# First batch of a Fourier-mixing kernel: six row chunks of 126 instead of eight of 95

## Chip, cores and metric

The kernel runs on one core of a Trainium2 chip. The metric is the device time of one execution in microseconds (us); the median of five runs is compared. The engines are called as the profile calls them: PE (TensorE matmul), PEld (its weight loads), DVE (VectorE), ACT (ScalarE), POOL (GpSimd), SP (SyncE, which here only issues transfers).

## What is computed

The real part of a two-dimensional Fourier transform of each of eight batches, and then a two-layer network with a leaky ReLU on every token. All is float32; the two weight matrices arrive as float64 and are converted on the chip.

```python
B, S, D, F = 8, 3008, 256, 2048
X = np.fft.fft(x, axis=1)             # x: (8, 3008, 256)
X = np.fft.fft(X, axis=2).real        # -> (24064, 256) tokens
h = X.reshape(B * S, D) @ w_in        # (256, 2048)
g = np.maximum(0.01 * h, h)
out = g @ w_out                       # (2048, 256)
```

## The kernel before

**Units and steps.** Output positions k along the sequence are split by parity; a unit is (batch, parity c), odd positions (c = 1) before even ones (c = 0): (0, 1), (0, 0), (1, 1) and so on. Each unit has three column blocks of about 251, and each block is raised to the hidden width and brought down again in eight steps. A step is `up` (`raised`: four matmuls of 251 columns, L738; `activate`: DVE L747, L751 and L752, ACT's leaky ReLU L753, and from the third block on four POOL operations, L760 to L763) and, three steps later, `down` (seven matmuls, L811; for the first two blocks eight plain ones, L791). The feature transform is folded into w_in (`fold_w_in`, L516).

**The sequence transform.** The rows of x are folded by symmetry on DVE (`add_mirrors` L287, `fold_columns` L294 and L296, `fold_halves` L303). Then each unit has a cosine and a sine part. In each, the even rows and the odd rows are multiplied with tables of cosines or sines, and a butterfly of sums and differences on DVE makes the tile `mix` that L738 reads. With 95 rows to a chunk x stands in eight chunks, four for the even and four for the odd rows. A third, small transform of eight columns does the Nyquist feature of all batches; its row is stored to DRAM (`store_nyquist`) and loaded back spread over all partitions (`nb`). It is transformed once for each parity.

**Two kinds of transform.** All units but the first run `fold_rows` (24 operations on DVE and four on ACT for both parts together) and then `dft`: `even_rows` and `odd_rows`, eight matmuls of about 95 columns (L572). The first unit, (0, 1), leaves out those folds: the class `Direct` multiplies the chunks with larger tables of their own (`even_rows` L390: 94, 94, 188 and 188 columns; `odd_rows` L399: four matmuls of 376 columns, for the two parts cut at column 251 into 251 and 125). Unit (0, 0) takes the first way; its two transforms stand in steps 18 and 21 (`step`, `f in (2, 5)`).

**Order at the start.** PE, DVE and SP run in an order written out by hand until step 15; after that a scheduler places the instructions. `keep_warm(n)` issues n matmuls of 256 columns on a blank tile. PE's order at the start: 16 keep_warm, `fold_w_in` (four matmuls, L516), even Nyquist rows, 3 keep_warm, even cosine rows, odd Nyquist rows, 3 keep_warm, even sine rows, odd rows of both parts (251 columns), `spread_first` (L706), two `raised`, odd rows (125 columns), and the first `down`. On DVE `o.begin()` (L463 and L464), the first operations on a freshly loaded piece of w_out, stands ahead of the butterflies of the odd rows; `o.end()` (L482) makes that piece ready for the first `down`.

**Transfers.** SP issues, in order: w_in, the Nyquist rows, x (even rows, two halves, with the feature table between), tables, x (odd rows, two halves, with tables between), tables, pieces of w_out and w_in, and the eight ordinary tables. After each `fold_w_in` piece one row of the result is spread into `wn` by four small transfers; those of the first piece go through ACT's queue, and L747 reads them. SP's and ACT's transfers take eight completion counters in turn, so the issue of one waits until the one that had its counter before has landed.

**Buffers.** The banks of tag "up" (four of 512 columns) hold the transforms' products and those of `raised`; x has one buffer, so batch 1 is loaded when unit (0, 0)'s products have read batch 0. The tags "s" (four buffers) and "g" (five) hold the direct tables at the start and the activations later.

Of the kernel before, what the change touches and what calls it, by code (L numbers as in the profile page):

```python
# [55 lines left out]
F32 = mybir.dt.float32  # L58
I32 = mybir.dt.int32
U32 = mybir.dt.uint32  # L60
ALU = mybir.AluOpType
# [3 lines left out]
P = 128  # L65
# [3 lines left out]
NT = 8  # L69
# [10 lines left out]

DW = [6 * KB[1], 8 * KB[1], 8 * KB[1]]

# [17 lines left out]


def k_order(c):


    if c == 1:
        below = 4 * np.arange(1, KB[1] + 1) - 1
        k = np.concatenate([below, S // 8 - below])
        return np.concatenate([k, Q - k])
    first = np.concatenate([8 * np.arange(KB[0]) + 2, [188], 8 * np.arange(23) + 4, 8 * np.arange(24)[::-1]])
    k = np.concatenate([first, S // 8 - first[first != 188]])  # L110
    return np.concatenate([k, Q - k[:-1]])


def laid_out(x):

    rows = row_order()
    none = rows < 0
    d = np.concatenate([np.arange(P + 1), np.arange(D - 1, P, -1)])  # L120
    x = np.concatenate([x, np.zeros((B, 1, D), x.dtype)], axis=1)

    def taken(rows, d):
        return x[:, np.where(none, S, rows % S)][..., d]

    mirrored = (D - d) % D
    x = np.stack([
        np.stack([taken(rows, d), taken(S - rows, mirrored)], axis=2),
        np.stack([taken(H - rows, d), taken(H + rows, mirrored)], axis=2),
    ], axis=2)  # L130
    nyquist = x[..., P].transpose(1, 2, 3, 4, 0).copy()
    x[..., P] = 0.0
    x = x.reshape(*x.shape[:4], 2, NT // 2, D).transpose(0, 2, 4, 1, 3, 5, 6)
    return x, nyquist


def seq_tables():


    out = np.zeros((4, 2, LOADED, TW[0][1]), np.float32)  # L140
    direct_out = np.zeros((2, LOADED, sum(DW)), np.float32)
    rows = row_order()

    def values(chunk, k):

# [16 lines left out]
    for part in range(2):  # L162
# [19 lines left out]
        out[2 * part + 1, 0, :, : TW[0][1]] = np.concatenate([values(4, fours)[part], values(4, eights)[part], p, q], axis=1)  # L182
        k = k_order(1)
        direct_out[part] = np.concatenate(
            [values(i, k[: KB[1] * (1 + i // 2)])[part] for i in range(4)] + [values(i, k)[part] for i in range(4, NT)], axis=1)
    return out, direct_out
# [52 lines left out]
def tile_fnet_leaky_relu(  # L239
    ctx: ExitStack,  # L240
    tc: tile.TileContext,
    x: bass.AP,
    x_nyq: bass.AP,
    w_in: bass.AP,
    w_out: bass.AP,
    seq_tab: bass.AP,
    direct_tab: bass.AP,
    angle_tab: bass.AP,
# [14 lines left out]
    def dft_ps():  # L263
        return up_ps("dft_ps")
# [14 lines left out]
    def load_rows(t, b, h, odd):  # L279
        nc.sync.dma_start(t[:, h, :, odd * NI[0] : NI[0] + odd * NI[1]], x[b, h, odd])  # L280

    zs = {}
# [51 lines left out]
    class Rows:  # L334
# [3 lines left out]
        def __init__(self, src, scratch, part, c):  # L338
            self.src, self.scratch, self.part, self.c = src[0:ROWS], scratch, part, c
# [40 lines left out]
    class Direct:  # L380


        def __init__(self, src, part, tab):
            self.src, self.part, self.tab, self.c = src[0:ROWS], part, tab, 1

        def even_rows(self, m):

            pe, n, at = dft_ps(), KB[1], 0
            for i, (lo, hi) in enumerate(((0, n), (n, 2 * n), (2 * n, 4 * n), (2 * n, 4 * n))):
                nc.tensor.matmul(pe[0:m, lo:hi], lhsT=self.src[:, i], rhs=self.tab[0][0:ROWS, at : at + hi - lo],  # L390
                                 start=(i == 0), stop=(i == 3), skip_group_check=True)
                at += hi - lo
            return pe

        def odd_rows(self, m, lo=0, hi=KW[1]):

            po, n = dft_ps() if m == P else sum_ps(), KW[1]
            for i in range(4):
                nc.tensor.matmul(po[0:m, 0 : hi - lo], lhsT=self.src[:, 4 + i],  # L399
                                 rhs=self.tab[1 + i // 2][0:ROWS, i % 2 * n + lo : i % 2 * n + hi], start=(i == 0), stop=(i == 3))  # L400
            return po
# [15 lines left out]
    nyx = const.tile([LOADED, 2, 2, NT, B], F32, name="nyx")  # L417
    nyz = const.tile([LOADED, 16, B], F32, name="nyz")
    angle = const.tile([LOADED, 6], F32, name="angle")
    inf = const.tile([P, 2], F32, name="inf")  # L420
# [155 lines left out]
    def butterfly(to, m, part, c, v=nc.vector, direct=False):  # L576
# [34 lines left out]
        def even(pe):  # L611
            if direct:
                e0, pe = copied(pe, 0, n)
                v.tensor_tensor(ab[0:m, 0:n], e0[0:m, 0:n], pe[0:m, n : 2 * n], op=ALU.add)
                either(ab[0:m, n : 2 * n], e0[0:m, 0:n], pe[0:m, n : 2 * n])
                v.tensor_tensor(ev[0:m, 0 : 2 * n], ab[0:m, 0 : 2 * n], pe[0:m, 2 * n : 4 * n], op=ALU.add)
                either(ev[0:m, 2 * n : 4 * n], ab[0:m, 0 : 2 * n], pe[0:m, 2 * n : 4 * n])
                return
# [15 lines left out]

        def added(po, lo=0, hi=kw):
            nc.vector.tensor_tensor(to[0:m, lo:hi], ev[0:m, lo:hi], po[0:m, 0 : hi - lo], op=ALU.add)

        def subtracted(po, lo=0, hi=kw):
            nc.vector.tensor_tensor(to[0:m, kw + lo : kw + hi], ev[0:m, lo:hi], po[0:m, 0 : hi - lo], op=ALU.subtract)

# [39 lines left out]

    def fold_nyquist():
        nc.gpsimd.tensor_tensor(nyb, nya, nyb, op=ALU.add)
        nc.gpsimd.tensor_tensor(nya[:, 1], nyb[:, 0], nyb[:, 1], op=ALU.subtract)
        nc.gpsimd.tensor_tensor(nya[:, 0], nyb[:, 0], nyb[:, 1], op=ALU.add)

# [156 lines left out]
    def step(at):  # L842
        if at < len(steps):
# [3 lines left out]
            b, c = units[n]  # L847
            if n == 0 and f in (2, 5):
                dft(units[1], f // 5)
            if 0 < n < len(units) - 1:  # L850
# [23 lines left out]
    with tc.manual_schedule(engines={mybir.EngineType.DVE, mybir.EngineType.PE, mybir.EngineType.SP}):  # L874
        with tc.manual_schedule(engines={mybir.EngineType.Pool, mybir.EngineType.Activation}):
# [6 lines left out]
            t = x_tile()  # L882
            evens, odds = slice(0, NI[0]), slice(NI[0], NT)


            touched = const.tile([P, 1], F32, name="touched")
            nc.scalar.dma_start(touched, x[0, 0, 0, :, 0, 0, 0:1])

            nc.scalar.activation(lrelu, inf[:, 0:1], ACT.Lrelu)
            w = load_w_in(0, WN)  # L890
            nc.sync.dma_start(nyx, x_nyq)
            load_rows(t, 0, 0, 0)
            nc.sync.dma_start(feat_sb, feat_tab.rearrange("(a p) n -> p a n", p=P))
            load_rows(t, 0, 1, 0)
            tables = [[work.tile([P, 2 * WN], F32, tag=tag, bufs=bufs, name="direct") for tag, bufs in (("s", 4), ("g", 5), ("g", 5))]
                      for _ in range(2)]

            def load_direct(part, pieces):
                for i in pieces:
                    at = sum(DW[:i])  # L900
                    nc.sync.dma_start(tables[part][i][0:LOADED, 0 : DW[i]], direct_tab[part, :, at : at + DW[i]])

            load_direct(0, (0,))
            load_rows(t, 0, 0, 1)
            load_direct(0, (1, 2))
            load_rows(t, 0, 1, 1)
            load_direct(1, range(3))
# [7 lines left out]
            convert(w)  # L915
            fold_nyquist()
            differences = work.tile([P, 2 * WN], F32, tag="s", bufs=4, name="differences")[0:LOADED].rearrange("p (c d) -> p c d", d=P)
            cosine, sine = (Direct(src, part, tables[part]) for part, src in enumerate((differences, t[:, 0, 0, :, P:D])))
            nyq = Direct(nya[:, 1], 0, tables[0])
            for h in range(2):  # L920
# [24 lines left out]
            made_nyq[0](even_nyq)  # L945
            keep_warm(3)
            made = [mix(u, part, direct=True) for part in range(2)]
# [3 lines left out]
            made_nyq[1](odd_nyq)  # L951
            keep_warm(3)
            made[1][0](sine.even_rows(P))
# [18 lines left out]
        with tc.manual_schedule(engines={mybir.EngineType.Activation}):  # L972
# [16 lines left out]
            convert_on(o2, o3)  # L989
            w2 += load_w_in(2 * WN, WN, (1,))  # L990
            o4, o5 = load_w_out(4), load_w_out(5)
            up(*steps[4])
# [10 lines left out]
            fold_w_in(2 * WN, WN, w2)  # L1003
            o6, o7 = load_w_out(6), load_w_out(7)
            for at, old, new in ((8, o4, o5), (9, o5, w3[0]), (10, w3[0], w3[1]), (11, w3[1], o6), (12, o6, o7), (13, o7, None), (14, None, None), (15, None, None)):
                if old is not None:
# [8 lines left out]
                else:  # L1015
                    down(*steps[at - 2])
                if at == 14:
                    nyq = Rows(nya[:, 0], [nyz], 0, 0)
                    nyq.fold_even(nc.gpsimd)
                    nyq.fold_odd(nc.gpsimd)  # L1020
                    for part in range(2):
                        fold_halves(t, part, 0, slice(0, NT))
        done = 14
        for part in range(2):
            fold_rows(units[1], part)
    nyq_t = nyquist_tile()
    for made, bank in zip(butterfly(nyq_t, B, 0, 0), (even_rows(nyq, B), odd_rows(nyq, B))):
        made(bank)
    store_nyquist(0, nyq_t)
    spread(units[1])  # L1030
    for f in range(0, NH, WB):
        combine_w_out(f)
# [35 lines left out]
```

## Time and profile before

| | |
|---|---|
| median of 5 runs | 1900.37 us (1899.68 to 1901.15) |
| the profiled execution | 1900.05 us |
| its span (first to last instruction) | 1898.3 us |
| busy: PE, PEld, DVE, ACT, POOL | 1892.2, 1684.7, 1283.5, 503.5, 1117.5 us |
| matmul records on PE | 9122 |
| granted PE clock over the span | 1.000 |
| moved by DMA | 78.33 MB, mean 41 GB/s |

A line of the timeline gives the start and the duration in us, the engine, the line of the kernel, the operation, the output and inputs by the program's names, the form, the number of records, and in brackets the idle time before it with what ended it. Times count from the start of the span. A line of the waits gives who waited for whom, the total in us, how often, and the longest. A line of a DMA queue gives packets, MB and the share of 16 engines' time. SPq and ACTq are the sequencers of SP and ACT, which issue transfers.

### The profile page before, as it was taken

How to read it: one execution, taken by the hardware profiler on the slowest of the kernel's cores; microseconds unless marked ns; L12 is line 12 of the kernel's file. 1: busy time of each engine (PE TensorE's matmuls, PEld its weight loads, DVE VectorE, ACT ScalarE, POOL GpSimd, SP SyncE). 2: the span in 40 equal slices, each digit the busy share in tenths (PEclk: the TensorE clock that was granted, in tenths of full speed). 3: DMA queues.
4: the chain of work that ended last, by engine and by line, in shares of the span. 5: the costliest groups of instructions: out<-in, count | busy, mean ns of one | idle time of the engine just before them, and what ended most of it. 6: DMA issues, size and time to landing. Idle time of an engine off the chain costs nothing.

```text
span 1898.3 us, 25339 instructions
## 1 busy us (share of the span) xinstructions
PE 1892.2 (100%) x9122; PEld 1684.7 (89%) x9122; DVE 1283.5 (68%) x2563; ACT 503.5 (27%) x682; POOL 1117.5 (59%) x1511
## 2 busy tenths in 40 slices
PE   9999999999999999999999999999999999999999
PEld 7888888988889888898888988888888888888988
DVE  8879765696656965569555796558865688555554
ACT  3532222232222322223222232222322223222222
POOL 2137655576555765558555675556655566555554
PEclk9999999999999999999999999999999999999999
DMA  7212000120002000020000200002000020000000
GB/s 279 78 32 108 12 20 23 38 82 12 31 12 93 27 23 20 12 108 13 21 20 12 108 23 12 19 12 108 23 12 20 13 117 12 20 12 23 12 11 23
DMA packets 33628, 78.33 MB, mean 41 GB/s; under 512 B 5456, under 2 KB 19536, under 8 KB 33504
## 3 DMA queue, kind: packets, MB, share of 16 engines
q1 hardware_dynamic: 32496, 76.45, 10.9%
q8 instruction: 73, 1.20, 0.3%
q14 instruction: 51, 0.42, 0.1%
q10 hardware_dynamic: 1008, 0.26, 0.1%
HBM read 51.99 MB, written 24.71 MB: 40 GB/s over the span
## 4 chain that ended last, share of the span: by engine, by line
PE 98%; DMA 1%; DVE 0%; SPq 0%; issue 0%; ACT 0%; DVEq 0%
PE sum_ps L811 58%; PE cos_ps L738 17%; PE sin_ps L738 17%; PE sum_ps L791 3%; PE dft_ps L572 3%; PE wf_ps L516 1%; DMA direct<-in_direct_tab_dram 1%; DMA xt<-in_x_dram 0%; PE dft_ps L399 0%; DVE xt L287 0%; SPq L280 0%; PE sum_ps L706 0%; SPq L449 0%; DVE differences L303 0%; DVE xt L294 0%
## 5 line engine op out<-in xcount | busy, mean ns | idle before, releaser
L753 ACT ACTIVATE g<-g 128x1004 f32<-128x1004 f32 (+1 forms) x384 | 399.9, 1041 | 1107.6 <-DVE g L752 1023.9
L747 DVE SCALAR_TENSOR_TENSOR cos<-nb,wn,cos_ps 128x251 f32<-128x251 f32 (+1 forms) x768 | 329.9, 469 | 518.1 <-PE cos_ps L738 516.0
L760 POOL TENSOR_TENSOR s<-g 128x251 f32<-128x251 f32 (+1 forms) x368 | 275.2, 748 | 652.5 <-ACT g L753 652.5
L811 PE MATMUL sum_ps<-s,wt 128*128 128x251 f32 (+1 forms) x2208 | 528.0, 374 | 0.0
L811 PEld LDWEIGHTS sum_ps<-s,wt 128*128 128x128 f32 x2208 | 415.4, 188 | 53.7 <-POOL s L761 1.0
L738 PE MATMUL cos_ps<-mix,wf 128*128 128x251 f32 (+1 forms) x1536 | 388.0, 375 | 0.0
L738 PE MATMUL sin_ps<-mix,wf 128*128 128x251 f32 (+1 forms) x1536 | 387.7, 374 | 0.0
L811 PE MATMUL sum_ps<-g,wo 128*128 128x251 f32 (+1 forms) x1472 | 372.9, 375 | 0.0
L738 PEld LDWEIGHTS cos_ps<-mix,wf 128*128 128x128 f32 x1536 | 291.2, 190 | 34.4 <-ACT power L465 0.5
L738 PEld LDWEIGHTS sin_ps<-mix,wf 128*128 128x128 f32 x1536 | 290.4, 189 | 34.7
L761 POOL TENSOR_TENSOR s<-s,g 128x251 f32<-128x251 f32 (+1 forms) x368 | 319.2, 867 | 0.0
L811 PEld LDWEIGHTS sum_ps<-g,wo 128*128 128x128 f32 x1472 | 277.2, 190 | 31.7
L763 POOL TENSOR_TENSOR s<-g,s 128x251 f32<-128x251 f32 (+1 forms) x368 | 277.7, 755 | 28.9
L751 DVE TENSOR_TENSOR g<-cos,sin_ps 128x502 f32<-128x502 f32 (+1 forms) x384 | 259.1, 675 | 42.7 <-DVE cos L747 8.0
L752 DVE TENSOR_TENSOR g<-cos,sin_ps 128x502 f32<-128x502 f32 (+1 forms) x384 | 256.8, 669 | 0.0
L762 POOL TENSOR_TENSOR s<-g 128x251 f32<-128x251 f32 (+1 forms) x368 | 255.5, 694 | 0.0
L811 PE MATMUL sum_ps<-g,wt 128*128 128x251 f32 (+1 forms) x736 | 215.8, 375 | 0.0
L811 PE MATMUL sum_ps<-s,wo 128*128 128x251 f32 (+1 forms) x736 | 215.8, 375 | 0.0
L811 PEld LDWEIGHTS sum_ps<-s,wo 128*128 128x128 f32 x736 | 139.5, 190 | 16.3
L811 PEld LDWEIGHTS sum_ps<-g,wt 128*128 128x128 f32 x736 | 139.8, 190 | 15.9
L835 DVE TENSOR_TENSOR o<-e,sum_ps 128x251 f32<-128x251 f32 (+1 forms) x180 | 65.9, 407 | 0.0
L572 PEld LDWEIGHTS dft_ps<-tab,xt 95*128 95x128 f32 x480 | 58.3, 192 | 1.4
(123 smaller groups left out, 850.0 us busy)
## 6 DMA issues: line engine op xcount, KB each, us to landing
xt<-in_x_dram SPq DMA_DIRECT2D x32, 1024.0 KB, 8.0
out_dram<-o SPq DMA_DIRECT2D x78, 251.0 KB, 2.6
raw<-in_w_in_dram SPq DMA_DIRECT2D x8, 512.0 KB, 4.7
raw<-in_w_out_dram SPq DMA_DIRECT2D x8, 512.0 KB, 4.6
out_dram<-o SPq DMA_DIRECT2D x16, 250.0 KB, 2.0
nb<-nyq_dram SPq DMA_DIRECT2D x8, 376.5 KB, 3.3
nb<-nyq_dram SPq DMA_DIRECT2D x7, 376.0 KB, 4.0
direct<-in_direct_tab_dram SPq DMA_DIRECT2D x4, 376.0 KB, 5.2
```

Of the source, the lines that this page charges most:

```text
L572: nc.tensor.matmul(o, lhsT=still, rhs=moving, start=(i == 0), stop=(i == 3), skip_group_check=True)
L738: nc.tensor.matmul(pt[blk][:, h * n : (h + 1) * n], lhsT=wf[:, blk, fs[h] * P : (fs[h] + 1) * P], rhs=mixed[b, c][blk][:, at : at + n], st ...
L747: nc.vector.scalar_tensor_tensor(cos[:, hs], in0=spreads[b, c][:, at : at + n], scalar=wn[:, fs[h] : fs[h] + 1], in1=pt[0][:, hs], op0=ALU ...
L751: nc.vector.tensor_tensor(g[:, 0], cos[:, 0 : 2 * n], pt[1][:, 0 : 2 * n], op=ALU.add)
L752: nc.vector.tensor_tensor(g[:, 1], cos[:, 0 : 2 * n], pt[1][:, 0 : 2 * n], op=ALU.subtract)
L753: nc.scalar.activation(g, g, ACT.Lrelu)
L760: nc.gpsimd.tensor_tensor(s1, a[1][0], a[1][1], op=ALU.add)
L761: nc.gpsimd.tensor_tensor(s2, s1, a[0][0], op=ALU.subtract)
L762: nc.gpsimd.tensor_tensor(s3, a[0][0], a[1][0], op=ALU.subtract)
L763: nc.gpsimd.tensor_tensor(s4, a[0][1], s2, op=ALU.subtract)
L811: nc.tensor.matmul(sums[j][p], lhsT=still[p], rhs=moving[p], start=(f == 0 and i % 2 == 0), stop=(f == NH - 1), skip_group_check=True)
L835: nc.vector.tensor_tensor(to, x, y, op=ALU.add)
```

## The change

Batch 0 gets a layout and tables of its own, separate from the other batches.

- Its rows stand in six chunks, three even and three odd, of up to 126 rows (the second and sixth chunk hold two halves of 64 partitions). A piece of x for it is 768 KB instead of 1024 KB. The Nyquist rows of all batches are loaded in the new layout for parity 1 (`nyf`, 96 KB), and in the old one, later, for parity 0 (`nyx`, 128 KB, behind w_out piece 7).
- `Direct` runs both units of batch 0. For unit (0, 1) `even_rows` has three matmuls (376, 188 and 188 columns) and `odd_rows` three of 376; its three tables per part have 752, 752 and 376 columns instead of 564, 752 and 752.
- Unit (0, 0) no longer runs `fold_rows` and `dft`. Per part it has `even_rows` (378, 189, 189 columns) and `odd_rows_even` (380, 188, 192), after one small fold (`fold_odd`). Its four tables (756 or 760 columns, about 379 KB each) are loaded between a w_in piece and w_out piece 4, into buffers of tag "s". Both parts' products now stand together, ahead of step 16, right behind the Nyquist product.
- The butterfly after `even_rows` has two operations instead of four in the direct form.
- keep_warm: none instead of three after the even Nyquist product, one instead of three after the odd one.

```diff
+FI, FROWS, FHALF = 3, 126, 64
-DW = [6 * KB[1], 8 * KB[1], 8 * KB[1]]
+DW = [[4 * 189, 4 * 95 + 4 * KB[0] + 4 * (KB[0] + 1)], [4 * 188, 2 * KW[1], KW[1]]]
...
         def even_rows(self, m):
-            pe, n, at = dft_ps(), KB[1], 0
-            for i, (lo, hi) in enumerate(((0, n), (n, 2 * n), (2 * n, 4 * n), (2 * n, 4 * n))):
-                nc.tensor.matmul(pe[0:m, lo:hi], lhsT=self.src[:, i], rhs=self.tab[0][0:ROWS, at : at + hi - lo],
-                                 start=(i == 0), stop=(i == 3), skip_group_check=True)
-                at += hi - lo
+            pe, n = dft_ps(), (KW[self.c] + 1) // 2
+            for i, (chunk, to) in enumerate(((1, pe[0:m, 0 : 2 * n]), (0, pe[0:m, 0:n]), (2, pe[0:m, n : 2 * n]))):
+                at, rows = (i + 1) * n if i else 0, slice(0, FROWS if i else P)
+                nc.tensor.matmul(to, lhsT=self.src[rows, chunk], rhs=self.tab[0][rows, at : at + to.shape[1]],
+                                 start=(i == 0), stop=(i == 2), skip_group_check=True)
             return pe
...
+        def fold_odd(self, scratch):
+            self.z = scratch
+            for i, op in enumerate((ALU.add, ALU.subtract)):
+                nc.vector.tensor_tensor(scratch[:, i], self.src[:, FI], self.src[:, FI + 1], op=op)
+
+        def odd_rows_even(self, m):
+            po, n, tab = dft_ps(), KB[0], self.tab
+            nc.tensor.matmul(po[0:m, 0:380], lhsT=self.src[:, FI + 2], rhs=tab[1][:, 0:380],
+                             start=True, stop=False, skip_group_check=True)
+            blocks = po[0:m, 0:380].rearrange("p (b n) -> p b n", b=4)
+            for i, (at, w) in enumerate(((0, n), (n, n + 1))):
+                first = 380 + i * 4 * n
+                nc.tensor.matmul(blocks[:, :, at : at + w], lhsT=self.z[0:FROWS, 1 - i if self.part == 0 else i],
+                                 rhs=tab[1][0:FROWS, first : first + 4 * w].rearrange("p (b n) -> p b n", b=4),
+                                 start=False, stop=(i == 1), skip_group_check=True)
             return po
...
             if direct:
-                e0, pe = copied(pe, 0, n)
-                v.tensor_tensor(ab[0:m, 0:n], e0[0:m, 0:n], pe[0:m, n : 2 * n], op=ALU.add)
-                either(ab[0:m, n : 2 * n], e0[0:m, 0:n], pe[0:m, n : 2 * n])
-                v.tensor_tensor(ev[0:m, 0 : 2 * n], ab[0:m, 0 : 2 * n], pe[0:m, 2 * n : 4 * n], op=ALU.add)
-                either(ev[0:m, 2 * n : 4 * n], ab[0:m, 0 : 2 * n], pe[0:m, 2 * n : 4 * n])
+                w = (kw + 1) // 2
+                e0, pe = copied(pe, 0, w)
+                v.tensor_tensor(ev[0:m, 0:w], e0[0:m, 0:w], pe[0:m, w : 2 * w], op=ALU.add)
+                either(ev[0:m, w:kw], e0[0:m, 0 : kw - w], pe[0:m, w:kw])
...
-            if n == 0 and f in (2, 5):
-                dft(units[1], f // 5)
...
             made_nyq[0](even_nyq)
-            keep_warm(3)
...
-            keep_warm(3)
+            keep_warm(1)
...
             w2 += load_w_in(2 * WN, WN, (1,))
+            even_tables = [[work.tile([P, 2 * WN], F32, tag="s", bufs=4, name="direct") for _ in range(2)] for _ in range(2)]
+            for part in range(2):
+                for i, at in enumerate((0, DW[0][0])):
+                    nc.sync.dma_start(even_tables[part][i][:, 0 : DW[0][i]], direct_even[part, :, at : at + DW[0][i]])
             o4, o5 = load_w_out(4), load_w_out(5)
...
             o6, o7 = load_w_out(6), load_w_out(7)
+            nc.sync.dma_start(nyx, x_nyq)
...
         done = 14
-        for part in range(2):
-            fold_rows(units[1], part)
...
     spread(units[1])
+    for part in range(2):
+        made = mix(units[1], part, direct=True)
+        made[0](evens[part].even_rows(P))
+        po = evens[part].odd_rows_even(P)
+        made[1](po)
+        made[2](po)
```

## The prediction

> **What bounds the kernel now.** The page first: TensorE, then its waits.
>
> ```profile
> PE 1892.2 (100%) x9122; PEld 1684.7 (89%) x9122; DVE 1283.5 (68%) x2563; ACT 503.5 (27%) x682; POOL 1117.5 (59%) x1511
> PE 98%; DMA 1%; DVE 0%; SPq 0%; issue 0%; ACT 0%; DVEq 0%
> PE sum_ps L872 <- POOL blank L877: 1.1, 1, 1.1
> PE dft_ps L399 <- DVE differences L303: 0.4, 1, 0.4
> ```
>
> PE is busy all through, and after its start it waits once, 0.4 us. So each matmul saved or added counts, as long as its operands keep up; only in the first 34 us is that in doubt. There the page's chain is a transfer of tables and one of x. Third, the timelines of the start: PE, then DVE.
>
> ```profile
> 14.63 1.13 PE L390 MATMUL dft_ps<-direct,nyx 95*8 95x94 f32 x8
> 15.69 1.56 PE L872 MATMUL sum_ps<-blank 128*128 128x256 f32 x6
> 18.27 2.69 PE L399 MATMUL sum_ps<-direct,nyx 95*8 95x376 f32 x8
> 20.89 1.56 PE L872 MATMUL sum_ps<-blank 128*128 128x256 f32 x6
> 23.97 1.96 PE L399 MATMUL dft_ps<-direct,differences 95*128 95x251 f32 x8 [0.43 <-DVE differences L303]
> 28.38 1.11 PE L738 MATMUL cos_ps<-mix,wf 128*128 128x251 f32 x4
> 33.91 3.64 PE L791 MATMUL sum_ps<-g,wo 128*128 128x251 f32 x16
> ...
> 21.24 1.23 DVE L287 TENSOR_TENSOR xt<-xt 128x1024 f32<-128x1024 f32 x1 [0.48 <-DMA xt<-in_x_dram]
> 26.58 0.42 DVE L463 TENSOR_SCALAR wo<-raw 128x512 int32<-128x512 int32 x1
> 33.07 0.69 DVE L482 SCALAR_TENSOR_TENSOR wo<-wo,power 128x512 f32<-128x512 f32 x1
> ```
>
> A matmul leaves two records. L482 ends at 33.77, and the first L791, which needs that weight, starts at 33.91: PE and DVE arrive together. PE being full hides that DVE is full too. Fourth, the waits of SP's queue in the first 60 us, and the packets in two windows:
>
> ```profile
> SPq L901 <- DMA wn<-wf: 3.2, 2, 2.0
> SPq L449 <- DMA wn<-wf: 0.9, 2, 0.7
> q10 hardware_dynamic: 11, 0.00, 0.2%
> q10 hardware_dynamic: 205, 0.00, 3.9%
> ```
>
> SP's later issues wait for tiny transfers wn<-wf (four of 128 elements) that ACT issues from 13.64. They reuse one of eight completion counters in turn. q10 is ACT's queue: 11 packets ran in 13 to 16.5 us, 205 in 16 to 19. The wn transfers landed at 19.06, 20.57, 21.59 and 22.18; behind the third stands the first w_out load (issued 21.61, landed 25.80), which L463 reads.
>
> **The start on PE.** Columns cost 1.69 ns in the 251-column matmuls (0.425 us each) and 1.68 in the 512-column ones; under 100 columns a matmul costs 0.22 us whatever its width. By differences of starts:
> - Even products: 752 columns in three matmuls instead of 564 in four. Nyquist 1.06 becomes 1.26, cosine 1.18 becomes 1.26, sine 1.25 stays: +0.3.
> - Odd products, three chunks for four: Nyquist 2.62 to 1.97; the two parts 1.80 and 1.79 to 1.33 each; the 125-column rests 0.89 to 0.67 twice: -2.0.
> - keep_warm: three go after the even Nyquist product (-1.40), two of three later (-0.93).
>
> Together -4.0; the wait of 0.43 goes too. PE could be 4.46 earlier at L791.
>
> **The start on DVE and the queues.** The folds do 768, 384 and 381 elements where they did 1024, 512 and 508 (pitches 1.27, 0.62, 0.65). From the same 10.23 (the weight conversion ahead is unchanged) I walk the new order with 0.96, 0.49 and 0.49, and with two 188-column operations instead of four per even part: DVE reaches L463's place at about 22.3 instead of 26.58. The last x load must land by about 18. The bytes ahead of and with it fall from 6538 to 5388 KB; these loads ran at about 400 GB/s in the windows, so 21.22 becomes 18.3. Fine.
>
> What is late next is the w_out load, because its predecessors in SP's queue wait for wn. PE makes wf at the same time as before (16 keep_warm, then L516), so ACT still issues wn from 13.64. Nearest rows: wn 3 landed just behind the last x load (21.59 after 21.22), as if served behind the bytes issued before it, so it moves with them to 18.7. A w_out load takes 4.6 us (page, median): lands 23.3. DVE waits 1.0 there, in order, and the butterflies queued behind L463, with everything PE then wants, wait with it. From L463 to the end of L482 is 7.19, less 0.3 of the 0.43 that DVE idled for ACT's nb copy. The weight is ready at 23.3 + 6.9 = 30.2 instead of 33.77: **3.6 earlier**. PE, 4.46 earlier if alone, waits 0.9. Bounds: 4.46, if the load lands by 22.3; and 1.1, if wn lands no earlier than before (load at 25.7, weight ready at 32.6).
>
> A rule speaks against my reading. The Trainium skill, DMA: Bandwidth & Descriptors, section "Queues, rings and completion order", says that each DMA engine takes turns between the queues it has work for, packet by packet. Then fewer bytes on SP's queue would not bring ACT's packets forward while SP's queue is still full, and the sum would take 1.1. The rows lean the other way: 11 of some 512 wn packets in the first window, though the transfers were issued early in it. Unloaded, at 51.80, a wn transfer took 2.0 us; here 5.4 to 6.7.
>
> The second half of the Nyquist row goes behind the table loads (landed 40.05; read by DVE at 40.16; its result had 0.7 to spare on PE). These loads end about 2.9 earlier, so it allows 3.6 as well.
>
> **Unit (0, 0).** Its two transforms took 1.75 each (PE 125.69 to 127.44; 141.84 to 143.60), eight matmuls of about 95 columns at 0.22. Now each part streams 378 + 189 + 189 + 380 + 188 + 192 = 1516 columns, six matmuls at 1.69 ns: 2.56. **+1.6** for both. By columns alone it would be 2.5; the old matmuls were at their floor, so part of the doubling is free.
>
> They also move ahead of step 16, back to back behind the Nyquist product: six banks through the four of tag "up". Walking DVE in the old time frame: PE ends the last odd product at 122.2. DVE, free of fold_rows, ends the Nyquist row at 119.3, the even butterflies at 122.0 (it waits for ACT's copy of the second), the first mix at 123.2, the second at 124.2. Step 16's sin matmul wants the first part's odd bank at 123.0: a wait of 0.2. The first mix also takes the buffer that held the Nyquist row, so it waits for that row's store: issued about 119.5, landed after about 2.3 (34.00 to 36.34 the first time) at 121.9, beside the 122.0. Bounds 0 and 1.5 (a store that takes the 3.7 of the nb load). I take **0.4**.
>
> **At nothing, with the cover.** Four even tables (1.5 MB) are issued ahead of w_out pieces 4 and 5: 3.9 us later at 400 GB/s, against 6.0 between landing (60.30) and use (66.31); without that cover DVE's conversion, and PE, would be late one for one. The buffers of tag "s" that they take are last read before 34. The reload of nyx stands behind w_out 7 and ahead of four wn loads: 128 KB, some 9 us before these. Folds at step 14: 2.7 us of DVE for 2.35, beside PE's L791. fold_rows, 24 operations on DVE and four on ACT between 113.7 and 118.4, goes: no gain, PE did not wait for it. Batch 1's x loads start after 122.2 instead of 143.80; the first pair needs 7.8 (143.80 to 151.58), so 130.6, and DVE's in-order queue meets its fold at 132.3. If it came later, step 19's activation behind it would slip; PE has 4 us more before it wants those banks.
>
> **Sum.** -3.6 + 1.6 + 0.4 = -1.6. The profiled execution took 1900.05 (span 1898.3, 1.75 around it): 1898.45; the median of the runs stands 0.32 above it, so **1898.8**.
>
> **The rivals.**
> - *The gate stands still* (0.24): wn lands as before, or the start does not deliver its bytes. -1.1 + 1.6 + 0.4 = +0.9: 1901.3. For it: the rule above. Against: the packet counts; and 3008-byte packets ran as fast per byte (120 ns) as 4096-byte ones (162), so fewer bytes are less time.
> - *Slower, at the bank wait* (0.15): the four direct products in a row are the place. DVE holds the first mix back (the Nyquist store, the copies on ACT), and PE stands before step 16's sin. Once that wait passes 2.0, all of the 3.6 is spent and the kernel is slower; at 4 it is 1902.4, and the 0.2% bound is passed at 5.8. For it: DVE runs 122 to 127 without a gap in my walk. Against: its rows there are all under 0.35 us.
> - *All of it* (0.06): the load lands by 22.3 and no bank wait: -4.46 + 1.6, 1897.5.
>
> The forecast's own case (advance of 2.5 to 4.4) has 0.55. Dropping keep_warm leaves PE waits of about 1 us, at a granted clock of 1.00 all along. TensorE: Matmul & The Clock Gate, Part 1, has the clock halve after an idle window of about 3.4 us; no wait above is that long, and the sum by it is the same.
>
> **Numbers.** Low 1897.2: all of it, less 0.3 for the runs' spread. High 1902.4: gate at 1.1 and a bank wait of 1.5. A difference of 0.2%, 3.8 us, is about what a measurement of this kernel can tell from no change. Faster by that would need more than PE can save at the start: 0.04. Slower by that needs a bank wait near 6, or an x fold that late: 0.08. Within: 0.88.
>
> **What would show it.** Right: PE's waits list gains one of about 1 us before the first w_out matmul (L863), which starts near 30.3; wn's third landing near 19; the four products at unit (0, 0) take 5.1 us; a wait under 1 us before L810 there; PE dense after. Wrong: the first L863 after 32 (gate), or over 2 us of PE wait behind the direct products.

## The result and the profile after

The changed kernel takes 1905.86 us (median of 21 runs, 1901.62 to 1907.46), the kernel before 1900.47 on the same chip: a ratio of 1.0023, 95% interval 1.0017 to 1.0029. The forecast was 1898.8, in 1897.2 to 1902.4. The loss of 5.4 us is small, but it is there, and with the other sign than the sum.

The profiled execution of the changed kernel took 1900.34 (span 1898.6), 5.5 less than its own median and all but equal to the 1900.05 of before: executions of this kernel differ by up to 7 us, as some waits come out longer in one than in another and TensorE runs at half its clock for a while in some, so that this trace shows which waits there are, but not how long they usually get.

The page and the waits list of the changed kernel:

```profile
PE 1889.1 (99%) x9088; PEld 1680.8 (89%) x9088; DVE 1271.2 (67%) x2543; ACT 501.9 (26%) x674; POOL 1115.1 (59%) x1510
PE 96%; DVE 2%; issue 1%; DMA 0%; ACT 0%; DVEq 0%; SPq 0%
```

```profile
PE cos_ps L810 <- DVE mix L701: 1.4, 1, 1.4
PE sum_ps L883 <- DVE o L907: 1.1, 1, 1.1
PE sum_ps L942 <- POOL blank L947: 1.1, 1, 1.1
PE sum_ps L863 <- DVE wo L543: 0.8, 1, 0.8
```

PE does 3.1 us less (1889.1 for 1892.2), but where it waited once after its start, 0.4 us, it now waits 1.4, 0.8 and 1.1. The chain of before had 98% on PE and under half a per cent on DVE; now 2% are DVE's. L883 is the matmul of the later blocks, L907 the sums that empty its banks; that wait lies near 171, where the forecast had "PE dense after".

The start, by the timelines of PE and DVE (start, duration, then the operation; in brackets the idle time before it and what ended it):

```profile
1.10 8.58 PE L942 MATMUL sum_ps<-blank 128*128 128x256 f32 x32 [1.10 <-POOL blank L947]
25.56 1.08 PE L810 MATMUL cos_ps<-mix,wf 128*128 128x251 f32 x4 [1.42 <-DVE mix L701]
31.30 3.64 PE L863 MATMUL sum_ps<-g,wo 128*128 128x251 f32 x16 [0.78 <-DVE wo L543]
```

```profile
24.33 0.43 DVE L524 TENSOR_SCALAR wo<-raw 128x512 int32<-128x512 int32 x1 [1.85 <-DMA raw<-in_w_out_dram]
```

The first w_out product starts at 31.30 for 33.91: 2.6 earlier. PE itself had a lead of 1.6 that is this execution's own, since its 16 keep_warm products took 8.58 us where those of before took 10.17 (the clock rose at 3.99 for 7.20); but that lead goes in the waits, as what comes last is the weight: in e11 below they took 9.96, and the product starts at 31.27 all the same. DVE stands 1.85 us before L524 for the w_out load, and the mix, queued behind, is late for PE.

Unit (0, 0), by PE's timeline:

```profile
114.74 1.55 PE L431 MATMUL dft_ps<-direct,xt 128*128 128x378 f32 x6
...
119.98 1.01 PE L810 MATMUL cos_ps<-mix,wf 128*128 128x250 f32 x4
```

The four products run from 114.74 to 119.98 and step 16 follows without a wait. The stretch before the late L883, by DVE's timeline of the changed kernel:

```profile
129.94 2.33 DVE L327 TENSOR_TENSOR xt<-xt 128x2048 f32<-128x2048 f32 x1
...
156.11 0.34 DVE L366 SCALAR_TENSOR_TENSOR xt<-xt,angle 95x128 f32<-95x128 f32 x1
156.37 0.75 DVE L367 SCALAR_TENSOR_TENSOR xt<-xt,angle 95x128 f32<-95x128 f32 x1
...
170.97 0.66 DVE L824 TENSOR_TENSOR g<-cos,sin_ps 128x502 f32<-128x502 f32 x1
171.55 0.40 DVE L907 TENSOR_TENSOR o<-e,sum_ps 128x250 f32<-128x250 f32 x1
```

and of the kernel before:

```profile
151.68 2.29 DVE L287 TENSOR_TENSOR xt<-xt 128x2048 f32<-128x2048 f32 x1 [1.72 <-DMA xt<-in_x_dram]
...
169.70 0.67 DVE L752 TENSOR_TENSOR g<-cos,sin_ps 128x502 f32<-128x502 f32 x1
170.29 0.40 DVE L835 TENSOR_TENSOR o<-e,sum_ps 128x250 f32<-128x250 f32 x1
```

Batch 1's x is folded from 129.94 on instead of 151.68, as its load comes earlier. With x folded, the scheduler puts the turns and folds of `fold_rows` for unit (1, 1) on DVE from 156.11 on, 25 operations that last 11.5 us, ahead of L907; the first product that reads them starts at 219.02. In the kernel before, the first of them (L326) started at 180.98, behind the sums L835. The windows of 127 to 174 (length, busy time and instructions of PE, PEld, DVE, ACT and POOL, then the granted clock, the DMA share and GB/s), first of the changed kernel, then of the kernel before:

```profile
127.00:174.00 47.00, 45.85 (x216) 40.41 (x215) 45.41 (x79) 17.16 (x30) 39.84 (x42) 1.00 0.24 78
```

```profile
127.00:174.00 47.00, 47.00 (x234) 42.41 (x233) 38.18 (x68) 11.87 (x18) 34.13 (x39) 1.00 0.31 117
```

DVE, 67% busy on the page, is 97% busy here: 45.41 of 47.00, for 38.18 before. It has hardly any slack left, so a delay there has nowhere to go but into the wait for L907.

### The profile page after: what moved, and what is told of

It reads as the page before. It is cut to its first block, busy times and chain, and to the rows that moved or that the text cites. A ratio compares the mean times of both kernels' runs of the same rounds, so it can differ in the third digit from the quotient of the medians.

```text
span 1898.6 us, 25262 instructions
## 1 busy us (share of the span) xinstructions
PE 1889.1 (99%) x9088; PEld 1680.8 (89%) x9088; DVE 1271.2 (67%) x2543; ACT 501.9 (26%) x674; POOL 1115.1 (59%) x1510
## 4 chain that ended last, share of the span: by engine, by line
PE 96%; DVE 2%; issue 1%; DMA 0%; ACT 0%; DVEq 0%; SPq 0%
PE sum_ps L883 56%; PE sin_ps L810 17%; PE cos_ps L810 17%; PE sum_ps L863 3%; PE dft_ps L633 3%; PE wf_ps L577 1%; DMA xt<-in_x_dram 0%; DVE cos L819 0%; DVE g L823 0%; DVE g L824 0%; DVE xt L367 0%; PE dft_ps L431 0%; DVE xt L366 0%; PE dft_ps L458 0%; DVE xt L343 0%
## 5 line engine op out<-in xcount | busy, mean ns | idle before, releaser
L819 DVE SCALAR_TENSOR_TENSOR cos<-nb,wn,cos_ps 128x251 f32<-128x251 f32 (+1 forms) x768 | 329.9, 469 | 527.3 <-PE cos_ps L810 525.0
L832 POOL TENSOR_TENSOR s<-g 128x251 f32<-128x251 f32 (+1 forms) x368 | 274.7, 746 | 653.2 <-ACT g L825 653.0
L883 PE MATMUL sum_ps<-s,wt 128*128 128x251 f32 (+1 forms) x2208 | 527.7, 374 | 0.0
L883 PEld LDWEIGHTS sum_ps<-s,wt 128*128 128x128 f32 x2208 | 415.7, 188 | 52.8 <-issue 0.3
L883 PE MATMUL sum_ps<-g,wo 128*128 128x251 f32 (+1 forms) x1472 | 372.9, 375 | 1.1 <-DVE o L907 1.1
L833 POOL TENSOR_TENSOR s<-s,g 128x251 f32<-128x251 f32 (+1 forms) x368 | 309.2, 840 | 0.0
L883 PEld LDWEIGHTS sum_ps<-g,wo 128*128 128x128 f32 x1472 | 277.3, 190 | 33.1 <-DVE o L907 1.5
L835 POOL TENSOR_TENSOR s<-g,s 128x251 f32<-128x251 f32 (+1 forms) x368 | 279.9, 761 | 28.9
L834 POOL TENSOR_TENSOR s<-g 128x251 f32<-128x251 f32 (+1 forms) x368 | 265.6, 722 | 0.0
L883 PE MATMUL sum_ps<-g,wt 128*128 128x251 f32 (+1 forms) x736 | 215.8, 375 | 0.0
L883 PE MATMUL sum_ps<-s,wo 128*128 128x251 f32 (+1 forms) x736 | 215.8, 375 | 0.0
L883 PEld LDWEIGHTS sum_ps<-s,wo 128*128 128x128 f32 x736 | 139.5, 190 | 16.3
L883 PEld LDWEIGHTS sum_ps<-g,wt 128*128 128x128 f32 x736 | 139.8, 190 | 15.9
L907 DVE TENSOR_TENSOR o<-e,sum_ps 128x251 f32<-128x251 f32 (+1 forms) x180 | 65.9, 407 | 0.0
L863 PE MATMUL sum_ps<-g,wo 128*128 128x251 f32 x256 | 57.2, 375 | 0.8 <-DVE wo L543 0.8
```

Source lines behind the costliest of these rows:

```text
L819: nc.vector.scalar_tensor_tensor(cos[:, hs], in0=spreads[b, c][:, at : at + n], scalar=wn[:, fs[h] : fs[h] + 1], in1=pt[0][:, hs], op0=ALU ...
L832: nc.gpsimd.tensor_tensor(s1, a[1][0], a[1][1], op=ALU.add)
L833: nc.gpsimd.tensor_tensor(s2, s1, a[0][0], op=ALU.subtract)
L834: nc.gpsimd.tensor_tensor(s3, a[0][0], a[1][0], op=ALU.subtract)
L835: nc.gpsimd.tensor_tensor(s4, a[0][1], s2, op=ALU.subtract)
L863: nc.tensor.matmul(sums[j][d][:, r * n : (r + 1) * n], lhsT=wo[:, fs[h] // NH, fs[h] % NH, d * P : (d + 1) * P], rhs=a[r][h], start=(f == ...
```

## The experiments

Two theories stood at first. A: the clock; without the five dropped keep_warm products PE idles at the start, and the granted clock falls in most executions. B: the waits themselves, of the late w_out load and of L907. The kernel before gave 1900.24 to 1900.51 beside each of the three groups of runs, so times can be compared across them.

**Group 1: the clock.** The changed kernel once more (e0); the five products put back (e1); the kernel before without them (e2); six products put where PE waits (e3).

> The changed kernel once more, unchanged. Its profiled execution was 1900.34 us at a granted clock of 1.000, its 21 timed ones had a median of 1905.86 at clocks of 0.997 to 1.000. Theory A (clock): PE stands or does little in the start (a wait of 1.4 us for mix, of 0.8 for the weight, small matmuls between them), and in most executions the granted clock falls to half for one or more stretches there; a profile of an execution of about 1905 shows a stretch of clock 0.5 between 15 and 60 us, 4 to 8 us long, and little else new. Theory B (order): the loss is waits, more of them when a transfer is late; the clock is a by-product; such a profile shows PE waits of 4 us or more behind 100 us.

```diff
             made_nyq[0](even_nyq)
+            keep_warm(3)
...
-            keep_warm(1)
+            keep_warm(3)
```

> The changed kernel with keep_warm(3) and keep_warm(3) at their two old places: five matmuls, 2.1 us of PE. Theory A: the clock stays at 1.000 as before the change; PE loses its waits of 2.2 us in exchange for the 2.1 us of matmuls, so the time falls to 1900.5 to 1902. Theory B: the five matmuls change nothing of what the waits wait for: 1904 to 1907, as the changed kernel.

```diff
             made_nyq[0](even_nyq)
-            keep_warm(3)
...
-            keep_warm(3)
+            keep_warm(1)
```

> The kernel before, with the five keep_warm matmuls taken out as the change does, and nothing else. PE then arrives 2.3 us earlier at products whose operands are not earlier, and waits instead. Theory A: the clock falls in most executions as in the changed kernel, 0.997 to 0.999, and the time is 1902 to 1906. Theory B: PE waits where it was busy, and the time stays within 1 us of 1900.5.

```diff
             spread_first(nyq_t)
+            keep_warm(4)
...
+            keep_warm(2)
             down(*steps[0])
```

> The changed kernel with keep_warm where PE waits: four matmuls (1.7 us) between the Nyquist spread and the first hidden-layer matmuls, two (0.85 us) ahead of the first w_out matmuls. They fill the waits of 1.4 and 0.8 us. Theory A: the clock stays at 1.000 and the time is 1899.5 to 1901.5, at or below the kernel with keep_warm at the old places. Theory B: 1904 to 1907.

Measured: e0 1904.72 (ratio to before 1.0020, 1.0012 to 1.0029); e1 1905.89 (1.0029, 1.0020 to 1.0038); e2 1902.39 (1.0014, 1.0005 to 1.0023); e3 1904.51 (1.0022, 1.0012 to 1.0031). The clock does fall, as two windows of e0 show:

```profile
24.27:27.68 3.41, 1.56 (x7) 0.98 (x6) 2.27 (x7) 1.44 (x3) 0.00 (x0) 1.00 0.96 319
27.68:31.09 3.41, 3.41 (x10) 2.76 (x9) 2.82 (x6) 0.78 (x3) 0.00 (x0) 0.50 1.06 387
```

After a window in which PE was busy for 1.56 of 3.41 us, the next 3.41 run at 0.50. In e2 four such stretches follow one another, and the kernel before loses 2.2 us (1902.39 against 1900.24 beside it) by dropping products whose absence the forecast counted as a gain of 2.3. But e1 and e3, which keep PE busy at the start and in whose traces the clock stays at 1.00, are no faster than e0. So a drop at the start does not explain the loss. The clock does go with the time of single executions: of the changed kernel's 22, the four listed with a granted clock of 1.000 took 1900.34 to 1902.66, the eleven with 0.997 or 0.998 took 1905.08 to 1907.30, and in e1, with the products back, the five under 1.000 still took 1906.36 to 1909.10. So part of the loss goes with the clock, and not only at the start. In the traces of e0, e1 and e3 one wait is common, for L907 near 172, 1.1 to 1.2 us; that pointed to B.

**Group 2: the waits one by one.**

```diff
-            o.begin()
             odd = [direct.odd_rows(P, *first) for direct in (cosine, sine)]
...
                     made[part][i](odd[part], *first)
+            o.begin()
```

> The first two operations of the w_out conversion (L524, L525) go behind the four mix operations of the direct products, so that the mix no longer waits for the w_out load. Theory of the late load: in the traces of the changed kernel the load landed at 24.3 to 25.7, DVE stood 1.85 us and more before L524, and PE waited 1.4 to 1.85 us before the first cos product and 0.78 before the first w_out product. With DVE free the mix ends about 1.5 us earlier, the cos wait falls under 0.3, the first w_out product comes 0.8 to 1.5 earlier, and the time falls by about 1, to 1903.5 to 1905; the 1.1 us wait for L907 near 172 stays. Theory of the clock: with the long wait gone no stretch at half clock follows, and the fast end of the runs shows more often, 1902 to 1903. Rival, nothing but the place of the wait: PE waits as much before the first w_out product instead, 1904.5 to 1906.

```diff
-    def load_x(b):
+    def load_x(b, after):
         t = x_tile()
+        if after is not None:
+            held = t[0:1, :, 0, 0 : NI[0] + 1 : NI[0], 0:1].rearrange("p h o d -> p h (o d)")
+            nc.scalar.copy(held, after[0:1, 0:4].rearrange("p (h o) -> p h o", h=2))
...
-                xs[b + 1] = load_x(b + 1)
+                xs[b + 1] = load_x(b + 1, None if b else hidden[steps[at - 2]][0])
```

> Batch 1's x load is held back to step 22 (about 145, where the kernel before had it at 143.8) by a copy of four elements on ACT into its buffer; the folds of x and the fold_rows behind it go back with it. Theory of the crowded DVE: the 1.1 to 1.2 us wait of PE for L907 near 172 goes, all else stays, the time falls by 1.1 to 1903.5 to 1905, and no other wait over 0.3 comes between 130 and 190. Rival: the wait belongs to the block's end and not to the folds; it stays, and the time with it (1904.5 to 1906).

```diff
-            fold_w_in(0, WN, w, "sum", queue=nc.scalar)
+            fold_w_in(0, WN, w, "sum", queue=nc.gpsimd)
```

> The four wn transfers of the first w_in piece leave ACT's queue and its completion counters and go out on GpSimd's queue; SP's loads behind them no longer wait for them. Theory of the late load: the last two table loads and the w_out load are issued by about 15.5 instead of 17.7 to 18.6 and the load lands by 21 to 22.5; DVE does not stand before L524, PE's waits before the first cos and the first w_out product go, and the first w_out product starts 1.0 to 2.5 earlier; the time falls by as much, to 1902 to 1904. If GpSimd takes some 1 us for each issue, its two Nyquist operations come 4 us later, still ahead of the place where PE wants that row. Rival, the load is late because of the bytes: it lands at 24 or later wherever it is issued, and nothing moves. Rival, wn itself lands too late (DVE wants it at 27.0): PE waits there instead.

> The same edit in the kernel before the change: the wn transfers go out on GpSimd's queue. There PE and DVE come to the first w_out product together (33.77 and 33.91), with the keep_warm products still in, so an earlier load can only bring what DVE's order gives: DVE works without idle from 10 to 27, so both theories expect no change over 0.5 us (1899.9 to 1900.8). If it is over 1 us faster, SP's waits for wn were a cost of the kernel before too, and the whole sum of the start was read wrongly.

Measured: e4 1904.88 (7 runs, 1900.61 to 1908.06; 1.0023, 1.0013 to 1.0034). The mix no longer waits and the first w_out product starts at 29.97, 1.3 earlier, but the median does not move. The profiled execution took 1907.07, and its trace shows where an execution of that length loses time. Its waits of PE, then its windows:

```profile
PE sum_ps L883 <- DVE o L907: 2.9, 1, 2.9
PE sum_ps L863 <- ACT g L825: 2.7, 1, 2.7
```

```profile
173.40:176.80 3.40, 0.58 (x3) 0.18 (x1) 3.40 (x8) 1.14 (x4) 2.47 (x4) 1.00 0.00 0
176.80:180.20 3.40, 3.35 (x8) 2.78 (x9) 3.40 (x10) 0.80 (x1) 2.44 (x4) 0.50 0.18 68
```

The wait for L907 is 2.9 here, and 3.41 us at half clock follow, which cost another 1.7: 4.6 in this one place. The 2.7 (at 40.4; DVE stood 3.77 us before L819 for the second half of the Nyquist row) was followed by the same 1.7 again (43.7 to 47.1 at 0.50). So in this trace the wait behind DVE comes first, and the clock falls after it.

e5, the late x load: 1900.31 (11 runs, 1898.31 to 1901.08; 0.9997, 0.9988 to 1.0005), 4.4 below e0 and 5.5 below the changed kernel's median. It was expected at 1903.5 to 1905, since only the 1.1 us of the profiled wait were counted. The wait for L907 is gone from its list; DVE's window:

```profile
127.00:174.00 47.00, 47.00 (x223) 41.87 (x223) 35.41 (x55) 14.33 (x21) 35.73 (x43) 1.00 0.33 124
```

e7, wn on GpSimd's queue: 1902.36 (1.0010, 1.0002 to 1.0019). The w_out load is issued at 11.86 and lands at 21.23, for 18.55 and 24.30 in the changed kernel; the first w_out product starts at 29.41. The wait for L907 is 3.2 in its trace. e10, the same edit in the kernel before: 1900.27 (0.9998, 0.9989 to 1.0007), no change, as both theories expected. There DVE had hardly any idle time to give.

**Group 3: order or transfer, and what is left.** e5 moved two things, the x load and what DVE does with it. e11 leaves the load and the folds of x early and holds back only `fold_rows`.

```diff
-        cos, sin = (angle[0:ROWS, 2 * a + i : 2 * a + i + 1] for i in range(2))
+        cos, sin = (turned[0][0:ROWS, 2 * a + i : 2 * a + i + 1] for i in range(2))
...
+    turned = [angle]
...
     def step(at):
+        if at == 29:
+            turned[0] = const.tile([LOADED, 6], F32, name="late")
+            nc.scalar.copy(turned[0][0:1, 0:1], hidden[steps[27]][0][0:1, 0:1])
+            nc.scalar.copy(turned[0], angle)
```

> Batch 1's x load stays early, at 120 to 139, and so do its folds; only the turns of fold_rows for unit (1, 1) are held back: from step 29 on they read their angles from a copy that waits for step 27's values, so that on DVE's queue they stand behind the output sums L907 instead of ahead of them. Theory of the order on DVE: the wait for L907 near 172 (1.1 to 3.2 us in the traces) goes as it did with the late x load, and the time with it: 1900 to 1901.5. Rival, the x load itself (its transfers between the stores of the first two blocks, DVE slowed beside it): the wait stays over 1 us, 1903.5 to 1906.

Measured: 1900.11 (11 runs, 1898.65 to 1901.48; 0.9999, 0.9990 to 1.0008), with x landing early all the same. DVE's timeline of e11:

```profile
167.92 0.41 DVE L908 TENSOR_TENSOR o<-e,sum_ps 128x250 f32<-128x250 f32 x1
168.27 1.26 DVE L908 TENSOR_TENSOR e<-e,sum_ps 128x250 f32<-128x250 f32 x3
...
175.09 0.61 DVE L366 SCALAR_TENSOR_TENSOR xt<-xt,late 95x128 f32<-95x128 f32 x1 [2.07 <-ACT xt L363]
```

The sums (L908 here) start at 167.92 instead of 171.55, the first turn at 175.09 instead of 156.11, and DVE even has idle time. PE's list has no wait for the sums:

```profile
PE sum_ps L947 <- POOL blank L952: 1.1, 1, 1.1
PE cos_ps L811 <- DVE mix L702: 0.9, 1, 0.9
PE sum_ps L864 <- DVE wo L544: 0.8, 1, 0.8
```

So it is the order on DVE's queue, not the transfer.

The three others build on e5: e14 puts the five keep_warm products back as e1 did, e8 adds the edit of e7, e9 adds that of e4 as well.

> The late x load with the five keep_warm products of the start put back (2.3 us of PE). Theory of the late w_out load: PE stood 1.8 and 0.8 us before the first cos and w_out products without them, so they fill idle time: the first w_out product moves by under 0.7 and the time is within 0.7 of the late x load's 1900.31. Theory of the clock: they also keep the granted clock up in the windows that hold the wait, so the upper end of the runs (1901.1 without them, listed clock 0.998) comes down and the median is 0.3 to 1 lower. Rival: the products cost what they last, 1902 to 1902.6.

> The late x load and the wn transfers of the first piece on GpSimd's queue together. Alone the one gave 1900.31, and in the other's trace the first w_out product came at 29.41 instead of 31.60. If the two add, the time is 1897.8 to 1898.8, the 1898.8 that the sum of the prediction came to. If the start's gain is lost again at the next weight piece (PE waited 1.1 us near 53.5 with the wn edit alone), 1899 to 1900.3.

> Both of these and the w_out conversion begun behind the mix as well. The load lands at about 21.2 there, ahead of the place where DVE wants it, so moving the conversion back has nothing to hide and makes the weight later by the 1.5 us of the mix on DVE at most: 1898 to 1900, no better than the two edits without it.

Measured: e14 1901.14 (1.0002, 0.9994 to 1.0011): the products cost some 0.8 of the 2.3 us that they last (the two intervals overlap), and the upper end of the runs, 1901.9, does not come down. The clock is not without effect in e5 (the five executions listed at 1.000 took 1898.31 to 1899.86, the six below it 1900.31 to 1901.08), but the products do not win that back. e8 1898.21 (11 runs, 1896.83 to 1899.13; 0.9988, 0.9980 to 0.9997): faster than both kernels. e9 1898.26 (0.9991, 0.9982 to 0.9999), no better than e8, as expected. In e8 DVE meets the w_out load without a wait:

```profile
22.66 0.40 DVE L527 TENSOR_SCALAR wo<-raw 128x512 int32<-128x512 int32 x1
```

## Where the prediction was right and wrong

**Wrong, and most of the miss of 7.1 us: "At nothing", batch 1's x.** The step asked whether the x load would be in time for its fold (130.6 against 132.3) and found that it was; the 4 us of cover that it counted were for a load that comes late. It did not ask what else would move up behind it. The scheduler places what is ready, so `fold_rows` of unit (1, 1), some 47 us from its use, went ahead of sums that PE needed at once. That term, taken at 0, measured 4.6 us (e0 less e11) to 5.75 (the changed kernel's median less e11): 1.1 to 3.2 of wait in the traces, and, as e4's windows show, 1.7 more where half clock follows. No trace was taken of an execution near the changed kernel's median, so how these parts share out there is not shown. A row to see it in was there: DVE's busy time in that stretch of the kernel before, 38.18 of 47.00, leaves 8.8 for the 11.5 us of `fold_rows`, other work that moves in or out aside.

**Wrong size: "The start on DVE and the queues".** The gate did move: the third wn transfer landed at 18.05 (18.80 in e0) for the 18.7 of the sum, and the w_out load was issued at 18.55 for 18.7. DVE came to L524's place at 22.5, for 22.3. The term that was mis-sized is the load itself, 4.6 us by the page's median, which took 5.75 (4.99 to 6.43 over the traces with this start); that other loads, held back by the same gate, went out around it would explain the length, but was not tried by itself. It landed at 24.3 to 25.7 for 23.3, and the advance of 3.6 became 2.6 in the changed kernel's trace, 2.6 in e11's, and 0.8 in e0's, which has the stretch at half clock. PE's wait, 0.9 in one place by the sum, was 1.4 before the first cos product and 0.8 before the w_out product. With the gate out of the way (e8) the first w_out product is 4.0 earlier than before the change (29.89 for 33.91), and the time is 1898.2, near the 1898.8 of the sum. That is in part luck: e8 loses 0.9 of the 4.0 again, as PE waits near 54.8 where the forecast has no wait (before it DVE waits 1.9 and 1.5 for the wn transfers of the second w_in piece). Waits of 0.6 to 1.1 of that kind stand in the traces of e1, e3, e7, e8, e9 and e14, and their cause was not looked into. The reading that fewer bytes ahead bring wn forward, against the turn-taking rule of the Trainium skill (DMA: Bandwidth & Descriptors, "Queues, rings and completion order"), came out: third landing at 18.04 to 19.36 in all traces of the changed start that leave wn on ACT's queue, 21.59 before; e0, where ACT issued wn from 13.64 as before, has 18.80. The rule itself is not refuted by that, as no run varied the bytes alone.

**Wrong reason: keep_warm.** The sentence that ends "no wait above is that long, and the sum by it is the same" rested on the Trainium skill (TensorE: Matmul & The Clock Gate, Part 1), which has the clock fall after an idle window. Here it fell after windows in which PE was busy for 1.56 or even 2.03 of 3.41 us (e0, e2), and each stretch at half clock costs 1.7, half of its 3.41. Ahead of the first w_out product this showed in one of eight traces of the changed start without the products, and e14 gained nothing by them, so it weighs little there; behind the wait for L907 it is part of the loss.

**Right: unit (0, 0).** 5.24 us for the forecast 5.1, and no wait before step 16 where the sum had 0.4. The rival of the bank wait had the right sign and the wrong place. **Right: the rest at nothing**, the even tables, the reload of nyx, and the folds at step 14: none of these shows in any list of waits. The second half of the Nyquist row landed at 37.92 for 40.05, 2.1 earlier where the forecast had about 2.9; PE did not wait for it here, but in e4, where it landed at 39.62, it is the wait of 2.7.

With the order on DVE mended, e5 and e11 stand 0.2 below the kernel before, which the runs can't tell from none; e8, with the load in time as well, 2.1 below. So the sum of -1.6 is about what the change gives with these two edits, and not what it gives as written.

## What to carry to other kernels

A transfer that comes earlier is not only cover: it makes its readers ready earlier, and a scheduler that goes by readiness may put them on an in-order engine ahead of work that is due now. For each step that moves forward, list what it releases and look at the order of instructions on the engine that must do it, in the stretch and not over the whole span. And a wait has not one length: the one for L907 was 1.1 in the first trace, 2.9 and 3.2 in others, so look at a second trace before a wait is priced.

## What the runs showed of the hardware

TensorE's granted clock fell to 0.50 for 3.41 us after windows that were only partly idle. The windows list of e2, the kernel before without five products, shows PE busy for 2.03 of 3.41 us ahead of the drop:

```profile
20.32:23.73 3.41, 2.03 (x11) 1.36 (x10) 2.85 (x6) 0.24 (x1) 0.27 (x1) 1.00 0.92 305
23.73:27.14 3.41, 3.33 (x8) 2.76 (x9) 3.34 (x10) 0.00 (x0) 0.00 (x0) 0.50 0.96 291
```

The changes of the clock stand on a grid of 3.41 us: from its first rise to its first drop, e0 has 20.48 us, six steps, and e4 37.55, eleven. In e7 the clock rose at 4.53, so that windows of the grid begin at 168.37 and 171.78. There a wait of 3.2 us fell across two windows, and no drop followed:

```profile
168.37:171.78 3.41, 1.77 (x9) 1.25 (x7) 3.41 (x10) 2.02 (x6) 2.87 (x4) 1.00 0.00 0
171.78:175.20 3.42, 1.86 (x8) 1.36 (x8) 3.42 (x11) 1.04 (x1) 1.69 (x3) 1.00 0.00 0
175.20:178.60 3.40, 3.40 (x18) 2.98 (x17) 3.40 (x9) 0.24 (x1) 1.67 (x3) 1.00 0.39 151
```

In e4 the wait of 2.9 fell into one window and a drop followed. So much the same wait can cost 1.7 us more or not, it seems by where it falls on a grid whose start differs from one execution to the next (the clock first rose anywhere from 3.99 to 7.20 us). Busy time alone does not set it: 2.03 us led to a drop, and 1.77 and 1.86 did not; what the gate counts stays open.
